# A planner's dependency on two bias additions is loosened, and its table of urgencies replaced

## The chip, the cores and the metric

The kernel runs on one core of one Trainium2 chip. The metric is device time in microseconds (us), start to end of one execution; lower is better. Three runs of the kernel before gave 688.78, 688.41 and 686.49 us, so its median is 688.41 us.

## The reference

Two layers are computed on 2048 tokens of 640 channels, both gated by a vector `c` (adaptive layer norm), everything in float32. Cut to what matters:

```python
mod = (silu(c) @ w_mod).reshape(1, 6, 1, 640)
sa, ca, ga, sb, cb, gb = (mod[:, i] for i in range(6))
h = layernorm(x) * (1 + ca) + sa                  # x is A_q
ks = short causal convolution of k, 4 taps per channel
kv = ks * v
y  = long causal convolution of kv with ssm_k, per channel, by FFT, + kv * ssm_D
x  = x + ga * (h * y)
h  = layernorm(x) * (1 + cb) + sb
r  = relu(h @ w1 + b1)                            # 640 -> 1728
x  = x + gb * ((r * r) @ w2 + b2)                 # 1728 -> 640
```

## The kernel before

**Two stages.** The first stage, the long convolution, goes over five blocks of 128 channels (index b, 0 to 4). For each block the keys and values are loaded (`kn`), turned on TensorE (`kt`, `vt`), put through the short convolution on VectorE (`ks`), multiplied (`km`) and stored to DRAM as `kv_d` (`kst`); from there they come back in another layout (`lx`) as the tile `p`, which has an `ssm_k` half as well (`lh`). Matmuls with constant matrices then do a Fourier transform in steps: `pa` (64 x 64 or 128 x 64 pieces of `p`), `x` and `h` (spectra), products on VectorE (`mul`), their sums on GpSimd (`comb`), the way back (`qp`, then turns `t`, then `y`), and the residual (`fin`). Blocks overlap: the loads and turns of block b+1 stand between the steps of block b. Early in the first stage twenty groups of four transposes of the identity (`warm`), which compute nothing, are laid between TensorE's steps.

The second stage, the MLP, goes over eight chunks of 256 tokens (index n, 0 to 7). `tokens(n)` loads a chunk (`lx1`), takes its statistics (`st2`), normalizes it on ScalarE into `mtmp` (`hat`, one instruction for each half of 128 tokens) and turns it into `xt`, split in a high and a low part, since matmuls run on a reduced float32 (`xt`; the low part is a subtraction on GpSimd, on VectorE for chunk 0). Then there are 14 steps f over the hidden size: five products each (`f1`), bias, ReLU and square (`mid`, on ScalarE and VectorE, split again into high and low parts in `hring` or `w_W`), and four products into accumulators (`f2`). At a chunk's end VectorE multiplies the accumulators by the gate row (`out`) and adds them to the chunk's tile `x_n`, one half on GpSimd (`out` 2), one on VectorE (`out` 5), and the result is stored. In chunk 0 the 28 weight tiles are loaded (`lw`) and split (`wh`, `wl`).

**The two additions.** The second bias is multiplied by the gate once, `row1b = b2 * gate` (`gb2row` in the trace), on GpSimd. For each chunk GpSimd then adds this row to both halves of the chunk's tokens, in place, so two instructions for each chunk, 128 x 640 each. The trace shows them as `x<-x,gb2row`. They need the chunk's tile and must follow the reading of it by `hat`; the chunk's end needs them.

**What sets the order.** Nothing in the code's text order does. Every operation is recorded as a node, a planner inside the kernel (`Graph.order`) lays the nodes in time by rough costs, and each engine's instructions are emitted in that order. The planner picks, for each engine that is free, the ready node with the highest priority. A node's priority is the number that the table `URGE` has for its key and its place among the nodes of that key, in tenths of a microsecond; nodes without a number get one from the longest way to the end:

```python
n.told = i < len(table)
if n.told:
    n.prio = table[i] / 10
elif self.urge:
    n.prio -= LAST
```

The table covers the first stage and chunks 0 and 1; chunks 2 to 7 go almost wholly without. A node is ready when its `deps` are done. Most of these follow from the tiles that it reads and writes; some are set by hand, and those stand in the planner alone. [...] The code around the change (`tokens(0)` has just been recorded, so that the nodes with key `("xt", 0)` are chunk 0's transposes and splits):

```python
tokens(0)
later = {}
g.key = ("gate", 0)
mul(pool, row1b, row1b, row0b)
...
            mlp_middle(n, f)
            if f == 5:
                later[n] = g.nodes[-1].id
            mlp_back(n, f)
        for i in range(2):
            add(pool, X1t[n][:, i], X1t[n][:, i], row1b)
            g.nodes[-1].deps.add(later[n])
        mlp_out(n)
```

All instructions of both stages are issued from one line of a recording helper, so the trace gives them the line L444, and one goes by tiles.

Of the kernel before, what the change touches and what calls it, by code (L numbers as in the profile page):

```python
# [509 lines left out]
def ssm_mlp_kernel(  # L510
# [115 lines left out]
    g = Graph()  # L626
# [672 lines left out]
    def mlp_out(n):  # L1299
# [18 lines left out]
        if n < NC - 1:  # L1318
# [4 lines left out]
        ("b1", 0): [-2365, -2340],  # L1323
        ("comb", 0): [-473, -502, -505, -495, -516, -519, -559, -570, -227, -556, -600, -613, -607, -628, -621, -650,
            -657, -619, -664],
        ("comb", 1): [-939, -957, -941, -936, -967, -960, -971, -1018, -1013, -1030, -1032, -1058, -1065, -1084,
            -1080, -1235, -1228, -1133, -1182],
        ("comb", 2): [-1531, -1509, -1534, -1503, -1541, -1517, -1569, -1576, -1562, -1588, -1581, -1664, -1671,
            -1654, -1685, -1720, -1678, -1734, -1727],
        ("comb", 3): [-1945, -1981, -1969, -1948, -1966, -2021, -2001, -1990, -2004, -2026, -2032, -2059, -2056,  # L1330
            -2070, -2077, -2114, -2087, -2146, -2179],
        ("comb", 4): [-2384, -2378, -2394, -2387, -2825, -2412, -2416, -2431, -2442, -2450, -2475, -2482, -2485,
# [20 lines left out]
        ("fin", 0): [-1310, -1315, -1318, -1350, -1314, -1428, -1337, -1414, -1254, -1442],  # L1353
        ("fin", 1): [-1431, -1464, -1462, -1427, -1692, -1600, -1595, -1879, -1615, -1849],
        ("fin", 2): [-1852, -1858, -1856, -1848, -1912, -2059, -1955, -1999, -1995, -1827],
        ("fin", 3): [-2265, -2269, -2294, -2272, -2613, -2487, -2340, -2688, -2418, -2124],
        ("fin", 4): [-2635, -2642, -2639, -2645, -2664, -2964, -2715, -2950, -2717, -2898],
        ("gate", 0): [-2564, -2502, -2637, -2440, -2414, -2474, -2517, -2568, -2317, -2487, -2228, -2585, -2263,
            -2706, -2724, -2574, -2734, -2916, -2675, -2677, -2682, -2674, -2694, -2780],
        ("gb", 0): [-211, -221, -242, -252],  # L1360
        ("gi", 0): [-526, -339, 54, -592],
        ("h", 1): [-562, -577, -577, -604, -544, -956, -1031, -1033, -1019, -1023, -984, -1044, -1018, -1065, -944,
            -1129],
        ("h", 2): [-1169, -1237, -613, -1243, -1508, -1521, -1527, -1538, -1545, -1554, -1569, -1580, -1604, -1637,
            -1653, -1678],
        ("h", 3): [-1792, -1806, -1792, -1823, -2055, -1837, -2083, -2013, -2007, -2041, -2381, -2052, -2098, -2090,
            -2131, -2113],
        ("h", 4): [-2339, -2359, -2077, -2371, -1728, -2394, -1997, -2422, -1925, -2461, -2522, -2477, -2223, -2175,
            -2642, -2513],
        ("hat", 0): [-2700, -3202],  # L1370
        ("hat", 1): [-3488, -3440],
        ("hat", 2): [-3500, -3500],
# [25 lines left out]
        ("kst", 0): [-51, -277, -247, -252],  # L1398
        ("kst", 1): [-491, -593, -651, -725],
        ("kst", 2): [-1168, -720, -144, -1300],  # L1400
        ("kst", 3): [-1404, -1579, -839, -1069],
        ("kst", 4): [-1816, -2000, -1443, -2127],
        ("kt", 0): [4270, 4415, 1158, 3311],
        ("kt", 1): [-384, -383, -561, -691],
        ("kt", 2): [-642, -830, -1372, -1354],
        ("kt", 3): [-1303, -1334, -1494, -1642],
        ("kt", 4): [-1672, -1771, -1868, -1988],
        ("lgb", 0): [-115, -181],
        ("lgi", 0): [-454, -549, -526],
# [203 lines left out]
    kn = {}  # L1613
# [127 lines left out]
    for n in range(NC):  # L1741
        for f in range(NF):
# [7 lines left out]
            if f == 5:  # L1750
                later[n] = g.nodes[-1].id
# [33 lines left out]
```

## Time and profile before

| | |
|---|---|
| median of 3 runs | 688.41 us |
| the profiled execution | 691.67 us, of which the span from first to last instruction is 689.9 us |
| TensorE (PE) busy | 661.6 us, 96% of the span, 6825 matmul instructions |
| VectorE (DVE), ScalarE (ACT), GpSimd (POOL) busy | 417.7, 314.1 and 263.1 us |
| granted TensorE clock | 0.992 |
| mean DMA rate | 105 GB/s, most of it in the first 260 us |

Times in the trace are us from the span's start. PE is the engine that ends last nearly everywhere. The first stage fills about the first 283 us, the MLP the rest; the slices of the profile show the DMA engines busy in the first and nearly idle in the second. "Idle before" in a row is the time in which an engine had nothing to run, with what ended it. SP is the queue that issues nearly all DMAs, in order.

### The profile page before, as it was taken

The numbers are of one execution on the slowest core, as the hardware profiler recorded it, in microseconds if no ns is written. First come the engines' busy times: TensorE is split into PE (matmuls) and PEld (weight loads), VectorE is DVE, ScalarE is ACT, GpSimd is POOL, SyncE is SP. The second block draws the span as 40 slices with busy tenths as digits, with TensorE's granted clock in tenths as the row PEclk, the third lists the DMA queues.
The fourth block names the chain that finished last, engine by engine and source line by source line (L and its number), as shares of the span: only waits on it lengthen the run. The fifth ranks groups of instructions, "written<-read, shape, count | busy, mean of one in ns | idle before, by whom it ended". The sixth has DMA issues, their size and how long they took to land.

```text
span 689.9 us, 16413 instructions
## 1 busy us (share of the span) xinstructions
PE 661.6 (96%) x6825; PEld 598.6 (87%) x6825; DVE 417.7 (61%) x810; ACT 314.1 (46%) x650; POOL 263.1 (38%) x332
## 2 busy tenths in 40 slices
PE   9998889999999899999999999999999999999996
PEld 8987589879879687799989999899899899899996
DVE  2768559789699486676456562654653562662542
ACT  2765748876656655556225242243232242242220
POOL 2439448868958385354022211311211220310110
PEclk9999999999999999999999999999999999999998
DMA  9897898998776364072020200110020110200011
GB/s 241 224 310 257 210 264 197 238 240 215 203 185 163 89 157 150 20 211 75 1 77 0 77 1 1 23 55 1 0 77 1 39 39 1 52 26 1 1 39 38
DMA packets 108430, 72.45 MB, mean 105 GB/s; under 512 B 48514, under 2 KB 95810, under 8 KB 108356
## 3 DMA queue, kind: packets, MB, share of 16 engines
q1 hardware_dynamic: 106304, 70.80, 39.1%
q8 instruction: 53, 0.87, 0.5%
q10 hardware_dynamic: 1988, 0.61, 0.4%
q14 instruction: 21, 0.17, 0.1%
q0 software_dynamic: 64, 0.01, 0.0%
HBM read 56.98 MB, written 14.42 MB: 103 GB/s over the span
## 4 chain that ended last, share of the span: by engine, by line
PE 82%; DVE 9%; DMA 4%; issue 2%; ACT 2%; DVEq 0%; SPq 0%; POOL 0%; ACTq 0%; POOLq 0%
PE ps L444 82%; DVE mtmp L444 3%; DVE KV L444 3%; DMA p<-kv_d 2%; DVE hring L444 1%; DMA kv_d<-KV 1%; DVE x L444 1%; DVE wx L444 1%; DMA x<-x_d 1%; DMA out_dram<-x 1%; ACT a L444 0%; DVE s L444 0%; ACT KV L444 0%; ACT mtmp L444 0%; DVE w_W L444 0%
## 5 line engine op out<-in xcount | busy, mean ns | idle before, releaser
L444 PE MATMUL ps<-xt,w_S 128*128 128x256 f32 (+1 forms) x935 | 175.9, 330 | 4.0 <-DVE mtmp L444 3.0
L444 PEld LDWEIGHTS ps<-xt,w_S 128*128 128x128 f32 x935 | 140.9, 188 | 18.7 <-DVE mtmp L444 5.0
L444 PE MATMUL ps<-w_S,hring 128*128 128x320 f32 x648 | 109.9, 311 | 0.0
L444 ACT ACTIVATE mtmp<-ps,b1t 128x256 f32<-128x256 f32 (+1 forms) x112 | 50.1, 471 | 123.8 <-PE ps L444 121.0
L444 PEld LDWEIGHTS ps<-w_S,hring 128*128 128x128 f32 x648 | 99.1, 188 | 2.1
L444 DVE TENSOR_TENSOR mtmp<-ps,mtmp 128x256 f32<-128x256 f32 (+1 forms) x99 | 40.2, 418 | 75.7 <-ACT mtmp L444 75.4
L444 PE MATMUL ps<-a,gb 128*64 128x128 f32 x1260 | 75.7, 275 | 2.0 <-ACT a L444 1.4
L444 PEld LDWEIGHTS ps<-a,gb 128*64 128x64 f32 x1260 | 69.2, 137 | 8.8 <-ACT a L444 1.9
L444 POOL TENSOR_TENSOR xt<-xfs,xt 128x256 fp32r<-128x256 f32 x35 | 28.0, 807 | 119.6 <-ACT xt L444 119.4
L444 PEld LDWEIGHTS ps<-cst,p 64*64 64x64 f32 (+1 forms) x1792 | 60.1, 137 | 11.0 <-issue 4.7
L444 PE MATMUL ps<-cst,p 64*64 64x64 f32 (+1 forms) x1792 | 65.3, 247 | 4.4 <-DMA p<-kv_d 2.2
L444 DVE TENSOR_TENSOR hring<-mtmp,hring 128x256 fp32r<-128x256 f32 x74 | 41.7, 570 | 45.4 <-ACT hring L444 44.8
L444 POOL TENSOR_TENSOR wx<-wx 128x256 f32<-128x256 f32 x80 | 59.0, 755 | 7.5 <-DVE wx L444 6.2
L444 ACT ACTIVATE hring<-mtmp 128x256 fp32r<-128x256 f32 x74 | 30.4, 415 | 68.0 <-PE ps L444 47.2
L444 POOL TENSOR_TENSOR x<-mtmp,x 128x640 f32<-128x640 f32 (+1 forms) x9 | 12.9, 1435 | 125.2 <-DVE mtmp L444 125.2
L444 ACT ACTIVATE a<-ps 128x512 f32<-128x512 f32 x72 | 41.1, 616 | 35.9 <-PE ps L444 35.7
L444 PE MATMUL ps<-w_S,w_W 128*128 128x320 f32 x312 | 53.4, 311 | 1.5 <-DVE w_W L444 1.5
L444 PEld LDWEIGHTS ps<-w_S,w_W 128*128 128x128 f32 x312 | 47.8, 188 | 2.7 <-DVE w_W L444 1.7
L444 DVE SCALAR_TENSOR_TENSOR mtmp<-mtmp 128x256 f32<-128x256 f32 x91 | 46.7, 527 | 1.6
L444 DVE TENSOR_TENSOR wx<-ps,wx 128x512 f32<-128x512 f32 x64 | 40.9, 682 | 8.6 <-PE ps L444 6.1
L444 PE MATMUL ps<-gi,wx 64*128 64x128 f32 x640 | 40.4, 277 | 2.4 <-DVE KV L444 1.5
L444 POOL TENSOR_TENSOR mtmp<-mtmp 128x256 f32<-128x256 f32 (+1 forms) x21 | 14.8, 707 | 71.3 <-ACT mtmp L444 71.3
(141 smaller groups left out, 1097.6 us busy)
## 6 DMA issues: line engine op xcount, KB each, us to landing
wm<-in_w_mod_dram SPq DMA_DIRECT2D x25, 320.0 KB, 4.7
p<-in_A_ssm_k_dram SPq DMA_DIRECT2D x20, 256.0 KB, 4.8
KV<-in_A_k_dram SPq DMA_DIRECT2D x20, 256.0 KB, 5.0
KV<-in_A_v_dram SPq DMA_DIRECT2D x20, 256.0 KB, 5.2
p<-kv_d SPq DMA_DIRECT2D x20, 256.0 KB, 4.9
xp<-in_A_q_dram SPq DMA_DIRECT2D x10, 512.0 KB, 7.3
q<-in_A_q_dram SPq DMA_DIRECT2D x7, 640.0 KB, 5.4
out_dram<-x SPq DMA_DIRECT2D x14, 320.0 KB, 3.8
```

The source lines that it names most:

```text
L444: fn(*real, **{k: a.real() if isinstance(a, View) else a for k, a in kw.items()})
```

## The change

In the planner, the two additions of chunks 0 and 1 now have chunk 0's last `xt` node as their extra dependency, the one that the product `b2 * gate` had already; those of chunks 2 to 7 have none beyond their data. And the table is replaced: every entry of the first stage and of chunks 0 and 1 has another number. No instruction is added, removed or altered; each engine has as many of each kind as before.

```diff
     URGE = {
-        ("b1", 0): [-2365, -2340],
+        ("b1", 0): [-2693, -1653],
...
     tokens(0)
-    later = {}
+    first = max(n.id for n in g.nodes if n.key == ("xt", 0))
     g.key = ("gate", 0)
     mul(pool, row1b, row1b, row0b)
-    g.nodes[-1].deps.add(max(n.id for n in g.nodes if n.key == ("xt", 0)))
+    g.nodes[-1].deps.add(first)
...
             mlp_middle(n, f)
-            if f == 5:
-                later[n] = g.nodes[-1].id
             mlp_back(n, f)
         for i in range(2):
             add(pool, X1t[n][:, i], X1t[n][:, i], row1b)
-            g.nodes[-1].deps.add(later[n])
+            if n < 2:
+                g.nodes[-1].deps.add(first)
         mlp_out(n)
```

What that does to the queues is shown at three places. The first is GpSimd's queue around the ends of chunks 1 to 3. `x_2_...` is the tile of chunk 2, `xt_...` the low parts of the next chunk's `xt` (`xt_4849` in the old rows and `xt_4838` in the new are chunk 3's), the 64-row product belongs to a chunk's last step. Before:

```order
L444 TENSOR_TENSOR xt_4849<-xfs,xt_4849 128x256 x5
L444 TENSOR_TENSOR mtmp<-mtmp 64x256
L444 TENSOR_TENSOR x_2_4436<-mtmp,x_2_4436 128x640
L444 TENSOR_TENSOR x_3_4736<-x_3_4736,gb2row 128x640 x2
L444 TENSOR_TENSOR xt_5332<-xfs,xt_5332 128x256 x5
```

Now:

```order
L444 TENSOR_TENSOR x_1_1729<-mtmp,x_1_1729 128x640
L444 TENSOR_TENSOR x_3_4737<-x_3_4737,gb2row 128x640 x2
L444 TENSOR_TENSOR xt_4838<-xfs,xt_4838 128x256 x5
L444 TENSOR_TENSOR mtmp<-mtmp 64x256
L444 TENSOR_TENSOR x_2_4380<-mtmp,x_2_4380 128x640
```

The two additions of chunk 3 stood behind the end of chunk 2, and stand now ahead of chunk 3's low parts. The same move is made in chunks 2 to 7.

The second place is GpSimd's queue at the start of the MLP; `mtmp<-mtmp` are the squares of chunk 0, `x_0` and `x_1` the tiles of chunks 0 and 1. Before:

```order
L444 TENSOR_TENSOR gb2row<-gb2row,gbrow 128x640
L444 TENSOR_TENSOR mtmp<-mtmp 128x256 x6
L444 TENSOR_TENSOR x_0_1734<-x_0_1734,gb2row 128x640 x2
L444 TENSOR_TENSOR mtmp<-mtmp 128x256
L444 TENSOR_TENSOR xt_3983<-xfs,xt_3983 128x256 x2
```

Now:

```order
L444 TENSOR_TENSOR gb2row<-gb2row,gbrow 128x640
L444 TENSOR_TENSOR x_0_1698<-x_0_1698,gb2row 128x640
L444 TENSOR_TENSOR mtmp<-mtmp 128x256 x3
L444 TENSOR_TENSOR x_0_1698<-x_0_1698,gb2row 128x640
L444 TENSOR_TENSOR mtmp<-mtmp 128x256 x4
L444 TENSOR_TENSOR x_1_1729<-x_1_1729,gb2row 128x640
```

One addition of chunk 0 stands now directly behind the product that makes the row, ahead of the first squares, and chunk 1's additions, which stood behind chunk 0's end, begin seven squares later.

The third place is SP's queue at the last return of `kv_d` in the first stage. `p_2004` and `p_2018` are block 4's tile, `w1s` and `w2s` weight tiles of the MLP, `xp` the tokens for the last residual. Before:

```order
L643 DMA xp_2819<-in_A_q_dram 64x16x128 x2
L643 DMA kv_d<-KV 128x512
L643 DMA p_2004<-kv_d 128x8x64
L643 DMA w1s_3032<-in_B_w_dram 128x5x128
L643 DMA w2s_3035<-in_B_w_dram 128x640
L643 DMA w1s_3039<-in_B_w_dram 128x5x128
L643 DMA w2s_3042<-in_B_w_dram 128x640
L643 DMA p_2004<-kv_d 128x8x64 x3
```

Now:

```order
L643 DMA xp_2828<-in_A_q_dram 64x16x128 x2
L643 DMA kv_d<-KV 128x512
L643 DMA p_2018<-kv_d 128x8x64 x2
L643 DMA w1s_3045<-in_B_w_dram 128x5x128
L643 DMA p_2018<-kv_d 128x8x64 x2
```

Three of the four weight loads that stood between the pieces of block 4's tile have moved behind them.

More of the change, by code (lines that the diff above doesn't have):

```diff
@@ L1356, in ssm_mlp_kernel @@
[L1356 to L1371, printed above, removed]
@@ new lines, in ssm_mlp_kernel @@
+        ("comb", 0): [-494, -492, -506, -496, -513, -574, -567, -557, -517, -550, -543, -580, -581, -610, -617, -654,
+            -647, -665, -672],
+        ("comb", 1): [-967, -969, -955, -962, -973, -1006, -974, -976, -1013, -1020, -1049, -1089, -1026, -1068,
+            -1075, -1133, -1110, -1140, -1183],
+        ("comb", 2): [-1511, -1507, -1554, -1500, -1561, -1521, -1514, -1547, -1586, -1603, -1596, -1624, -1617,
+            -1664, -1671, -1721, -1691, -1731, -1697],
+        ("comb", 3): [-1962, -1958, -2102, -1972, -1979, -2006, -1999, -2049, -2021, -2027, -2034, -2083, -2076,
+            -2114, -2090, -2133, -2148, -2167, -2174],
@@ new lines, in ssm_mlp_kernel @@
+        ("gate", 0): [-2556, -2379, -2601, -2383, -2017, -2372, -2468, -2375, -1518, -2386, -2436, -2282, -568,
+            -2698, -2756, -3279, -2650, -3370, -2198, -2478, -3317, -2161, -2380, -2800],
+        ("gb", 0): [-165, -107, -114, -202],
+        ("gi", 0): [-685, -691, -535, -673],
+        ("h", 1): [-582, -593, -591, -674, -937, -953, -959, -968, -974, -985, -991, -1011, -1042, -1053, -1059,
+            -1085],
+        ("h", 2): [-1268, -1266, -1939, -1299, -928, -1510, -940, -185, -924, -530, 210, -1624, -1365, -1630, -1209,
+            -1658],
@@ new lines, in ssm_mlp_kernel @@
+        ("h", 3): [-1520, -1816, -2446, -1973, -1514, -1839, -1488, -1954, -1514, -1567, -1955, -2048, -1725, -2379,
+            -2183, -2190],
+        ("h", 4): [-2654, -2393, -1746, -2379, -1327, -2384, -1117, -2423, -1016, -2454, -1015, -2472, -2262, -2491,
+            -1311, -2510],
+        ("hat", 0): [-2737, -2671],
+        ("hat", 1): [-2828, -2815],
+        ("hat", 2): [-3500, -3500],
[25 rows of a table added]
+        ("kst", 0): [1094, 1317, 2035, 1095],
+        ("kst", 1): [-449, -685, -602, -754],
+        ("kst", 2): [-1024, -1161, -1264, -1313],
@@ new lines, in ssm_mlp_kernel @@
+        ("kst", 3): [-1498, -1274, -1334, -1698],
+        ("kst", 4): [-1433, -1853, -1806, 63],
+        ("kt", 0): [1434, 403, 69, -1119],
+        ("kt", 1): [84, -1026, 160, -738],
+        ("kt", 2): [-788, -813, 23, 251],
+        ("kt", 3): [-2561, -1184, -2302, -3670],
+        ("kt", 4): [-1294, -1552, -1525, -1507],
+        ("lgb", 0): [-16, -140],
+        ("lgi", 0): [-483, -533, -450],
[36 rows of a table added]
+        ("lxp", 0): [-935, -693],
+        ("lxp", 1): [-1111, -1033],
+        ("lxp", 2): [-1516, -1471],
@@ new lines, in ssm_mlp_kernel @@
+        ("mul", 2): [-1484, -1491, -1495, -1496, -1546, -1515, -1568, -1561, -1582, -1594, -1651, -1644, -1665,
+            -1658, -1674, -1688],
+        ("mul", 3): [-1951, -1944, -1968, -1960, -1986, -1402, -1999, -2006, -2072, -2049, -2083, -2087, -2128,
+            -2122, -2136, -2146],
+        ("mul", 4): [-2394, -2358, -2377, -2402, -2413, -2414, -2431, -2437, -2456, -2435, -2498, -2501, -2497,
+            -2511, -2532, -2530],
+        ("out", 0): [-3285, -3502, -3349, -3278, -3262, -3274, -3664, -3740],
[8 rows of a table added]
@@ new lines, in ssm_mlp_kernel @@
+        ("pac", 4): [-2660, -2360, -2295, -2321, -2134, -2329, -2252, -2259, -2541, -2541, -2461, -2272, -2372,
+            -2346, -2235, -2241],
+        ("pra", 0): [-1074, -1085, -1091, -1047, -1089, -1059, -1064, -1067, -1288, -1157, -1162, -1042, -1069,
+            -1107, -1118, -1064],
+        ("pra", 1): [-1173, -1294, -1183, -1152, -1372, -1315, -1310, -1298, -1305, -1289, -1206, -1206, -1347,
+            -1352, -1339, -1252],
+        ("pra", 2): [-1576, -1615, -1581, -1662, -1579, -1621, -1573, -1639, -1611, -1712, -1606, -1620, -1607,
+            -1704, -1576, -1577],
@@ new lines, in ssm_mlp_kernel @@
+        ("pra", 3): [-2007, -2027, -1997, -1993, -2002, -2032, -2059, -2021, -2075, -2079, -2054, -2020, -2037,
+            -2070, -2084, -2121],
+        ("pra", 4): [-2185, -2256, -2260, -2164, -2195, -2195, -2148, -2408, -2170, -2180, -1990, -2168, -2232,
+            -2190, -2215, -1912],
+        ("prm", 0): [-1131, -1056, -1293, -1147],
+        ("prm", 1): [-1383, -1343, -1281, -1405],
+        ("prm", 2): [-1613, -1725, -1742, -1734],
+        ("prm", 3): [-2061, -2032, -2166, -2099],
@@ new lines, in ssm_mlp_kernel @@
+        ("prm", 4): [-1989, -2157, -1919, -1951],
+        ("prp", 0): [-1248, -1116, -1312, -1160],
+        ("prp", 1): [-1446, -1442, -1324, -1450],
+        ("prp", 2): [-1757, -1773, -1885, -1805],
+        ("prp", 3): [-2129, -2071, -2194, -2197],
+        ("prp", 4): [-2278, -2220, -2260, -2281],
+        ("qp", 0): [-600, -632, -584, -610],
+        ("qp", 1): [-777, -1185, -935, -970],
+        ("qp", 2): [-1514, -1827, -1900, -2372],
+        ("qp", 3): [-1759, -1969, 921, -291],
+        ("qp", 4): [-2166, -2698, -3288, -3008],
@@ new lines, in ssm_mlp_kernel @@
+        ("qpc", 0): [-298, -540, -660, -666, -671, -675, -703, -910],
+        ("qpc", 1): [-1037, -1019, -1178, -1214, -1151, -1167, -1228, -1238],
+        ("qpc", 2): [-1599, -1587, -1675, -1681, -1748, -1754, -1762, -1768],
+        ("qpc", 3): [-1914, -2244, -1962, -1968, -2026, -2032, -2132, -2144],
+        ("qpc", 4): [-2652, -2509, -2319, -2570, -2732, -3291, -2489, -2585],
[26 rows of a table added]
+        ("warm", 0): [1525, 1417, -573, -129, -715, 1521, 1524, 1103, 16, -618, -234, 1526, -230, -642, 1413, 1532,
[38 rows of a table added]
```

99 lines of the change are left out of this document (19 added, 80 removed), and 356 rows, old and new, of the table URGE.

## The prediction

> **What bounds the kernel now.** I read the page first, then the busy time by stretches of 20 us, then the chain of waits and the timeline at the stretches with gaps.
>
> ```profile
> span 689.9 us, 16413 instructions
> ...
> PE 661.6 (96%) x6825; PEld 598.6 (87%) x6825; DVE 417.7 (61%) x810; ACT 314.1 (46%) x650; POOL 263.1 (38%) x332
> ...
> PE 82%; DVE 9%; DMA 4%; issue 2%; ACT 2%; DVEq 0%; SPq 0%; POOL 0%; ACTq 0%; POOLq 0%
> ```
>
> TensorE is the bound almost throughout: 82% of the chain that ended last is its own work. The change removes no instruction, so it can win only in the 689.9 - 661.6 = 28.3 us in which PE had nothing to run, or lose by adding to them. Where these stand:
>
> ```profile
> 60.00:80.00 20.00, 16.55 (x179) 13.02 (x180) 16.69 (x40) 14.89 (x27) 14.11 (x18) 1.00 0.87 271
> 80.00:100.00 20.00, 16.53 (x189) 12.95 (x189) 9.57 (x19) 9.89 (x20) 6.33 (x14) 0.91 0.98 248
> ...
> 220.00:240.00 20.00, 17.42 (x476) 13.32 (x476) 9.80 (x17) 13.81 (x31) 9.07 (x9) 0.91 0.49 121
> ...
> 280.00:300.00 20.00, 19.17 (x144) 18.02 (x143) 13.06 (x21) 13.86 (x30) 9.01 (x9) 1.00 0.24 64
> ...
> 340.00:360.00 20.00, 18.55 (x114) 16.84 (x113) 11.28 (x20) 4.55 (x12) 4.96 (x3) 1.00 0.19 49
> ...
> 440.00:460.00 20.00, 19.58 (x119) 17.54 (x118) 14.60 (x33) 7.10 (x16) 5.44 (x3) 1.00 0.23 66
> ...
> 480.00:500.00 20.00, 18.93 (x118) 17.39 (x116) 10.85 (x17) 4.41 (x11) 5.03 (x3) 1.00 0.00 1
> 500.00:520.00 20.00, 19.43 (x125) 18.14 (x126) 9.91 (x29) 7.04 (x17) 2.29 (x3) 1.00 0.24 66
> ...
> 540.00:560.00 20.00, 19.13 (x116) 17.19 (x115) 12.34 (x31) 6.70 (x15) 4.66 (x3) 1.00 0.24 67
> ...
> 580.00:600.00 20.00, 19.69 (x121) 17.80 (x119) 10.73 (x20) 4.40 (x11) 5.45 (x3) 1.00 0.10 21
> 600.00:620.00 20.00, 19.64 (x127) 18.34 (x128) 12.21 (x33) 8.70 (x20) 3.35 (x4) 1.00 0.15 47
> ```
>
> The columns are PE, weight load, DVE, ACT, POOL. Idle PE is 20 less the first: 3.45 and 3.47 us at 60 to 100, 2.58 at 220, and in the MLP, from 340 on, 1.45 + 0.42 + 1.07 + 0.57 + 0.87 + 0.31 + 0.36 = 5.05 us, all at ends of chunks; its other stretches are nearly full.
>
> **The chunks' ends (the dependency).** The group of additions, and one chunk's end, with rows of PE, DVE and POOL only:
>
> ```profile
> L444 POOL TENSOR_TENSOR x<-x,gb2row 128x640 f32<-128x640 f32 x16 | 28.9, 1828 | 0.0
> ```
>
> ```profile
> 492.19 2.13 DVE L444 SCALAR_TENSOR_TENSOR mtmp<-mtmp 128x256 f32<-128x256 f32 x2
> 492.42 1.62 POOL L444 TENSOR_TENSOR x<-mtmp,x 128x640 f32<-128x640 f32 x1 [16.31 <-DVE mtmp L444]
> ...
> 494.00 3.46 POOL L444 TENSOR_TENSOR x<-x,gb2row 128x640 f32<-128x640 f32 x2
> 494.24 3.50 DVE L444 TENSOR_TENSOR hring<-mtmp,hring 128x256 fp32r<-128x256 f32 x2
> ...
> 499.31 0.42 DVE L444 TENSOR_TENSOR w_W<-mtmp,w_W 128x256 fp32r<-128x256 f32 x1
> ...
> 500.12 0.62 PE L444 MATMUL ps<-xt,w_S 128*128 128x512 f32 x2 [1.19 <-DVE mtmp L444]
> ```
>
> The additions never wait once they are at the queue's head (idle 0.0): they run behind the chunk's last sum on POOL. While they run, VectorE's two subtractions take 3.50 us where one alone takes 0.42, so each addition holds VectorE by 3.50 / 2 - 0.42 = 1.33 us, and PE then waits 1.19 us for VectorE. The sum ahead of them (492.42) does the same once, and it stays. Sixteen additions hold VectorE at worst by 16 x 1.33 = 21 us; at the ends the price to PE is the 5.05 us. The new order takes the additions of chunks 1 to 7 away from there. Two of three holds go, and as PE's cover takes up the first of them, I take 4.0 of the 5.05 as gone; the ends of the range are 5.05 and 1.0.
>
> Where they go, beside the next chunk's turns:
>
> ```profile
> 400.40 1.73 ACT L444 ACTIVATE mtmp<-x,nm,rs 128x640 f32<-128x640 f32 x2
> ```
>
> ```profile
> 403.28 0.54 DVE L444 TENSOR_SCALAR xfs<-ps,cbs 128x256 f32<-128x256 f32 x1 [1.72 <-PE ps L444]
> ...
> 406.33 0.54 DVE L444 TENSOR_SCALAR xfs<-ps,cbs 128x256 f32<-128x256 f32 x1 [0.62 <-PE ps L444]
> ```
>
> ```profile
> 404.36 0.74 POOL L444 TENSOR_TENSOR xt<-xfs,xt 128x256 fp32r<-128x256 f32 x1 [13.78 <-ACT xt L444]
> ```
>
> The first addition can start when the first `hat` ends, 400.40 + 1.73 / 2 = 401.3, and two of 1.62 (the sum's row) end at 404.5, where the first low part started at 404.36; POOL had been idle for 13.78 us. So the low parts hardly move, and queued behind the additions is nothing else. VectorE has gaps of 1.72 and 0.62 us there, which take up one hold of 1.33 each in part. I charge 1.0 in all, some 0.2 us for each of the six chunks and so near the lower end, as both gaps are close to a hold's size; the range is from 0 to 6 x (2 x 1.33 - 1.72) = 5.6. Term: -4.0 + 1.0 = -3.0, from -5.0 to +4.6.
>
> The Trainium skill (SBUF — State Buffer, Who interferes with whom) says that a VectorE instruction with two SBUF inputs and a GpSimd instruction that reads SBUF block each other wholly, whichever comes first, and that one with at most one SBUF input, outside VectorE's two-port modes, doesn't contend. The 3.50 us agree for the two-input subtraction, and moved additions would by that rule hold VectorE as long at the new place as at the old; the term would then be -4.0 + 5.6 = +1.6, if no gap took any of it. That case is among the rivals, worked out there from rows.
>
> **The start of the MLP.**
>
> ```profile
> 276.13 0.69 DVE L444 TENSOR_TENSOR up<-ps,up 128x512 f32<-128x512 f32 x1 [0.72 <-PE ps L444]
> ...
> 278.31 0.62 DVE L444 COPY wx<-ps 128x512 f32<-128x512 f32 x1
> ...
> 282.43 1.54 POOL L444 TENSOR_TENSOR gb2row<-gb2row,gbrow 128x640 f32<-128x640 f32 x1 [0.28 <-ACT gbrow L444]
> 283.31 0.94 DVE L444 TENSOR_TENSOR xt<-xfs,xt 128x256 fp32r<-128x256 f32 x1 [0.63 <-ACT xt L444]
> ...
> 284.31 3.95 PE L444 MATMUL ps<-xt,w_S 128*128 128x256 f32 x31 [0.47 <-DVE xt L444]
> ```
>
> In the new order VectorE's half of the first `hat` stands ahead of the product and the copy of the first two rows (0.69 + 0.62 = 1.31 us) and of statistics of chunk 1. So the 0.83 us that PE lost at 280 to 300 can go, and about as much ahead of it: -1.7 at best. Against this, an addition follows the row's product at once: two holds more for the low parts on VectorE, 2 x 1.33 = +2.7 at worst. PE has `f1` of three steps to run in any order meanwhile, which hides most. I take -1.0, nearer the gain.
>
> **Block 4's last pieces.**
>
> ```profile
> 226.08 1.63 PE L444 MATMUL ps<-cst,p 64*64 64x64 f32 x96
> ...
> 230.41 0.88 PE L444 MATMUL ps<-ident,q 128*128 128x128 f32 x6 [2.34 <-issue]
> ```
>
> PE stood for 2.34 us with no data missing, just after it had run 96 instructions in 1.63 us. I read this as instructions that came late. The new SP order has three weight loads fewer in the burst of transfers there and puts the small matmuls less densely. Gain 0 to 2.34; I take 1.2, the middle.
>
> **Block 1's return from DRAM.**
>
> ```profile
> 69.28 1.10 PE L444 MATMUL ps<-ident,KV 128*128 128x128 f32 x8
> ...
> 70.31 2.06 PE L444 MATMUL ps<-gi,wx 64*128 64x128 f32 x32
> ```
>
> ```profile
> 72.05 0.40 DVE s L444
> ...
> 73.88 0.80 DVE s L444 x2
> ...
> 75.50 4.51 DMA kv_d<-KV
> ...
> 80.03 7.39 DMA p<-kv_d
> ...
> 87.46 8.94 PE ps L444 x128
> ```
>
> The last piece of block 1 must be turned (69.28), convolved, stored (75.50) and fetched again (80.03) before PE can go on at 87.46; this is the largest single wait, and no cover is left on PE. The new PE order puts these turns behind the matmuls of 70.31, so they start 2.06 to 2.9 us later; VectorE's queue in turn no longer has statistics between the convolution's steps (0.40 + 0.80 us and two short sums). With 2.06 - 1.2 and a little less waiting ahead of it I take +0.4, from -1.2 to +2.9.
>
> **Shape changes.** The PE queue changes matmul shape 121 times, it was 103.
>
> ```profile
> 15.07 1.29 PEld L444 LDWEIGHTS ps<-ident,KV 128*128 128x128 f32 x12 [0.17 <-issue]
> ```
>
> Each change leaves weight loading idle for up to 0.17 us; I take 0.1 of 0 to 0.17. Twelve of the 18 stand ahead of 48 us, among the `warm` transposes that fill waits there, so I count six: +0.6, up to 18 x 0.17 = +3.1. The Trainium skill (TensorEngine Tiling (Array Packing), Key Properties) speaks against the change here: a change of the tiling mode drains TensorE. It gives no time; with a drain of 0.17 us at all 18 the sum below would be 2.5 us higher.
>
> The rest of the first stage and of chunks 0 and 1 is reordered too; PE has the same work there ahead of each landmark (first `x` of each block, first `f1`). I count 0, and 3 us to both sides.
>
> **The sum.** -3.0 - 1.0 - 1.2 + 0.4 + 0.6 = -4.2 us. The profiled execution took 691.67 us, 3.3 above the median of 688.41; on it this gives 687.5, on the median 684.2, which is my number. About 0.3%, or 2.1 us, is what a measurement of this kernel can tell from no change.
>
> **The rivals.**
>
> *The holds are only moved (chance 0.17).* The last sum on POOL, which stays, holds VectorE by itself at each end, and only 1.0 of the 5.05 us goes: term 0, sum -1.2, 687.2 us. For it: the 1.62 us row has VectorE at 2.13 for two instructions. Against: the worse holds are the additions'.
>
> *VectorE is held beside the turns, and PE waits there (0.14).* Each pair costs 2 x 1.33 = 2.7 us on VectorE, the gaps take up 1.72 or 0.62, mean 1.2; the 1.5 left reach PE in chunks 2 to 7: +9.0 in place of +1.0. Sum +3.8, 692.2 us. It decides against the change from about 1.2 us a chunk on (6 x 1.2 + the other terms = +2). For it: the accumulator banks that the turns need are freed by these very VectorE instructions. Against: the two gaps, and that the matmuls behind VectorE have a queue of other work there.
>
> *Blocks 1 and 2 return late (0.11).* The turns behind `qp` cost their full 2.9 us at block 1, and as much at block 2: +2.5 + 2.9, sum +1.2, 689.6 us; with shape changes at 0.17, 692.
>
> *All of it goes well (0.04).* The ends give 5.05 with no new cost, block 4 all 2.34: about 680.
>
> My forecast has 0.54. So faster by over 0.3%: 0.54 + 0.04 = 0.58; within: 0.17 and half of the third rival, 0.22; slower: 0.14 and the other half, 0.20. The range reaches from 678, where all terms are at their best ends (-5.0 - 1.7 - 2.34 - 1.2 + 0 = -10.2), to 692.5, the second rival.
>
> **What would show it.** In the profile after, additions stand at about 401 to 405 and beside each later chunk's turns; at the chunks' ends VectorE's subtractions are back to 0.42 but for one beside the last sum, and idle PE from 340 us on falls from 5 to about 2. If instead `f1` or the turns wait for VectorE just behind the additions, the second rival holds. The first `f1` starts at 281 to 284; if it starts after 286 the first stage is what failed. At 228 the gap of 2.34 has shrunk; the first `pa` of block 1's `p<-kv_d` comes within a microsecond or two of 87.5. I am wrong if PE's idle time grows in stretches of which I said nothing.

## The result, and the profile after

The kernel after takes 683.31 us in the median of 7 runs (681.87 to 684.53), the kernel before 688.54 us on the same chips (7 runs, 684.40 to 690.43): ratio 0.993, with a 95% interval of 0.9903 to 0.9956. That is 5.2 us less, where 4.2 was forecast. The profiled execution took 684.05 us, span 682.2.

The head of the page of the kernel after, and its busy time by stretches of 20 us (PE, weight load, DVE, ACT, POOL, granted clock, DMA share, GB/s):

```profile
span 682.2 us, 16444 instructions
...
PE 659.1 (97%) x6825; PEld 595.3 (87%) x6825; DVE 415.2 (61%) x810; ACT 315.9 (46%) x650; POOL 260.8 (38%) x332
```

```profile
60.00:80.00 20.00, 17.81 (x208) 14.48 (x206) 14.32 (x32) 14.28 (x26) 15.03 (x18) 1.00 0.92 292
80.00:100.00 20.00, 18.94 (x257) 15.02 (x258) 11.99 (x24) 12.75 (x24) 9.07 (x16) 1.00 0.98 260
...
200.00:220.00 20.00, 17.16 (x273) 15.52 (x274) 16.91 (x26) 10.36 (x22) 12.27 (x17) 1.00 0.56 129
220.00:240.00 20.00, 19.91 (x575) 15.84 (x572) 16.97 (x24) 16.67 (x35) 14.99 (x14) 1.00 0.40 93
...
280.00:300.00 20.00, 18.42 (x138) 17.43 (x137) 12.92 (x20) 11.68 (x26) 11.48 (x12) 1.00 0.31 86
...
340.00:360.00 20.00, 20.00 (x125) 18.47 (x124) 11.44 (x29) 7.08 (x16) 3.94 (x3) 1.00 0.24 67
...
480.00:500.00 20.00, 20.00 (x125) 18.55 (x124) 10.35 (x23) 4.92 (x12) 1.68 (x1) 1.00 0.18 40
```

From 340 us on no stretch has idle PE any more until the last matmul; the 5.05 us are gone. At 280 to 300 idle PE has nearly doubled, from 0.83 to 1.58 us. In the first stage the idle time at 60 to 100 has fallen from 6.92 to 3.25 us, the gap at 220 is gone, and there is a new one at 200.

A chunk's end in the kernel after (the timeline of DVE and POOL; the same end that the prediction shows):

```profile
488.94 2.12 DVE L444 SCALAR_TENSOR_TENSOR mtmp<-mtmp 128x256 f32<-128x256 f32 x2
490.99 0.75 DVE L444 TENSOR_TENSOR hring<-mtmp,hring 128x256 fp32r<-128x256 f32 x2
491.66 0.88 DVE L444 TENSOR_TENSOR mtmp<-ps,gbrow 128x320 f32<-128x320 f32 x2
```

```profile
489.10 1.68 POOL L444 TENSOR_TENSOR x<-mtmp,x 128x640 f32<-128x640 f32 x1 [16.32 <-DVE mtmp L444]
```

The two subtractions take 0.75 us, they took 3.50. The sum on POOL still holds VectorE once (2.12 for two instructions), and no PE wait follows. The additions now wait for their chunk's `hat` and stand beside the turns (`xfs` are turned values that VectorE takes from PSUM):

```profile
398.24 3.12 POOL L444 TENSOR_TENSOR x<-x,gb2row 128x640 f32<-128x640 f32 x2 [14.01 <-ACT mtmp L444]
401.32 0.92 POOL L444 TENSOR_TENSOR xt<-xfs,xt 128x256 fp32r<-128x256 f32 x1
```

```profile
399.79 0.55 DVE L444 TENSOR_SCALAR xfs<-ps,cbs 128x256 f32<-128x256 f32 x1 [1.98 <-PE ps L444]
400.25 0.42 DVE L444 TENSOR_TENSOR mtmp<-ps,mtmp 128x256 f32<-128x256 f32 x1
400.58 1.06 DVE L444 TENSOR_TENSOR hring<-mtmp,hring 128x256 fp32r<-128x256 f32 x1
401.57 1.29 DVE L444 SCALAR_TENSOR_TENSOR mtmp<-mtmp 128x256 f32<-128x256 f32 x2
```

Here a pair holds VectorE by 1.06 - 0.42 = 0.64 us, not by two times 1.33: in its first two microseconds VectorE waits for PE or reads PSUM, and those instructions run at their plain 0.55 and 0.42. The row behind (1.29 for two, 0.75 plain) starts at 401.57, when the pair has ended (398.24 + 3.12 = 401.36), and stands beside GpSimd's low part of `xt`, which held VectorE in the kernel before too:

```profile
404.41 0.97 DVE L444 TENSOR_TENSOR hring<-mtmp,hring 128x256 fp32r<-128x256 f32 x1
```

**Which part of the kernel gained.** I cut each trace at two points: the start of the first `f1` of chunk 0, and that of chunk 3.

| trace | first `f1` at | from there to chunk 3 | from chunk 3 to the last `f2` |
|---|---|---|---|
| before | 283.33 | 133.69 | 266.57 |
| after | 281.06 | 133.57 | 261.55 |
| dependency alone | 280.48 | 138.10 | 261.44 |
| urgencies alone | 280.82 | 134.08 | 269.70 |
| before, chunks 2 to 7 freed | 279.43 | 134.54 | 261.37 |
| before, POOL's queue alone | 278.28 | 135.33 | 261.25 |
| after, chunks 0 and 1 later | 281.29 | 132.34 | 261.51 |

The last column splits the kernels cleanly: about 261.4 us wherever the additions of chunks 2 to 7 are free, 266.6 or more where they aren't (the 269.70 come from a profiled execution that took 692.48 us, 3.6 above its kernel's median; a stop of 1.44 us in it is followed by a granted clock of 0.66 at 510 to 515). The first column doesn't split them by table.

### The profile page after: what moved, and what is told of

It is laid out like the page before. It is cut to its first block, busy times and chain, and to the rows that moved or that the text cites. A ratio compares the mean times of both kernels' runs of the same rounds, so it can differ in the third digit from the quotient of the medians.

```text
span 682.2 us, 16444 instructions
## 1 busy us (share of the span) xinstructions
PE 659.1 (97%) x6825; PEld 595.3 (87%) x6825; DVE 415.2 (61%) x810; ACT 315.9 (46%) x650; POOL 260.8 (38%) x332
## 4 chain that ended last, share of the span: by engine, by line
PE 73%; DVE 5%; POOL 3%; issue 1%; ACT 1%; DMA 1%; SPq 0%; DVEq 0%; POOLq 0%
PE ps L444 73%; DVE wx L444 1%; DVE KV L444 1%; POOL wx L444 1%; DMA w2s<-in_B_w_dram 1%; POOL kover L444 1%; DVE xt L444 1%; DVE up L444 1%; ACT up L444 0%; DVE x L444 0%; POOL xp L444 0%; POOL KV L444 0%; ACT KV L444 0%; DVE w_S L444 0%; SPq L643 0%
## 5 line engine op out<-in xcount | busy, mean ns | idle before, releaser
L444 PE MATMUL ps<-a,gb 128*64 128x128 f32 x1260 | 77.3, 275 | 8.2 <-DVE wx L444 2.7
L444 DVE TENSOR_TENSOR hring<-mtmp,hring 128x256 fp32r<-128x256 f32 x74 | 37.0, 503 | 53.5 <-ACT hring L444 53.1
L444 PEld LDWEIGHTS ps<-cst,p 64*64 64x64 f32 (+1 forms) x1792 | 58.2, 135 | 10.8 <-issue 4.2
L444 POOL TENSOR_TENSOR x<-x,gb2row 128x640 f32<-128x640 f32 x16 | 26.1, 1648 | 88.2 <-ACT mtmp L444 73.2
L444 DVE SCALAR_TENSOR_TENSOR mtmp<-mtmp 128x256 f32<-128x256 f32 x91 | 43.4, 490 | 1.8
```

The lines of the kernel that those rows point to most:

```text
L444: fn(*real, **{k: a.real() if isinstance(a, View) else a for k, a in kw.items()})
```

## The experiments

**The dependency alone.** Old table, new dependency.

```diff
-            g.nodes[-1].deps.add(later[n])
+            if n < 2:
+                g.nodes[-1].deps.add(first)
```

> The kernel before with its old table and the new dependency alone; its queues are those of before up to the first steps of chunk 0. Theory A (two separate gains: the additions at the chunks' ends cost PE some 5 us, and the new table's first stage brings the MLP forward by 2.3): this one has the first alone, first f1 at 283.3 as before, idle PE from 340 us on near 0, 688.5 - 5.0 = 683.5, ratio 0.993 of before. Theory B (the gain is the table's, which orders the first stage and chunks 0 and 1 more densely; the holds were covered): 688.5, ratio 1.000, and idle PE from 340 us on stays near 5. By the prediction's own sizes (4.0 gone, 1.0 new) 685.5, ratio 0.996.

Measured: 687.91 us against 687.60, ratio 1.0007 (0.9991 to 1.0024). Neither theory had this. The last column of the table has its whole gain of 5.1 us, and the column before it gives 4.4 back, at the MLP's start. PE and ACT there, then the same stretch by fives:

```profile
291.71 2.35 PE L444 MATMUL ps<-xt,w_S 128*128 128x256 f32 x18
296.47 0.69 PE L444 MATMUL ps<-ident,mtmp 128*128 128x128 f32 x2 [2.41 <-ACT mtmp L444]
```

```profile
292.35 0.40 ACT L444 ACTIVATE hring<-mtmp 128x256 fp32r<-128x256 f32 x1
295.28 0.74 ACT L444 ACTIVATE w_S<-w2s 128x640 fp32r<-128x640 f32 x1 [2.53 <-DMA w2s<-in_B_w_dram]
295.94 0.47 ACT L444 ACTIVATE mtmp<-ps,b1t 128x256 f32<-128x256 f32 x1
```

```profile
290.00:295.00 5.00, 4.06 (x32) 3.69 (x31) 4.48 (x5) 2.66 (x5) 2.71 (x2) 1.00 0.40 101
295.00:300.00 5.00, 3.53 (x15) 3.51 (x16) 2.94 (x6) 3.30 (x8) 0.61 (x1) 0.66 0.79 219
```

It isn't a hold. The old table's numbers for the additions of chunks 0 and 1 were harmless while the old dependency kept them back; without it three of the four stand among the MLP's first steps on GpSimd, and ScalarE's queue now has splits of weights ahead of steps of `mid` that stood ahead of them (because the planner reckons with later squares on GpSimd, I suppose). One of them waits 2.53 us for its weight to land; PE's next turn of chunk 1 waits for the `mid` behind it (for the bank that it frees, I take it), and PE stops 2.41 us. In the five microseconds behind the stop the granted clock is 0.66. With chunks 2 to 7 freed alone (below), ScalarE waits nearly as long for a weight, two splits further on in its queue, and PE doesn't stop:

```profile
298.01 0.74 ACT L444 ACTIVATE w_S<-w2s 128x640 fp32r<-128x640 f32 x1 [2.37 <-DMA w2s<-in_B_w_dram]
```

**The urgencies alone.** New table, old dependency.

```diff
-            if n < 2:
-                g.nodes[-1].deps.add(first)
+            g.nodes[-1].deps.add(later[n])
```

> The new table with the old dependency: the first stage is that of after, the additions of each chunk stand again behind the sum of the chunk ahead of it. Theory A: first f1 at about 280 to 281, idle PE from 340 us on 4 to 5 us, 688.5 - 2.3 = 686.2, ratio 0.997. Theory B: 683.3 as after, ratio 0.993. If the dependency and the table only work together, this and the one with the dependency alone are both near 1.000.

Measured: 688.84 us, ratio 1.002 (1.0 to 1.004). Both theories fall: the table alone brings nothing. The idle PE from 340 us on is back at the ends (1.36 at 340, 1.10 at 480, 1.91 at 500). And the 2.3 us by which the profile of after was ahead at the first `f1` weren't the table's: six traces with the old first stage start it at 278.28 to 283.33 (mean 279.95), six with the new one at 277.67 to 281.60 (mean 280.43). The profile of before was the latest of all twelve.

**Only chunks 2 to 7 freed, old table.**

```diff
-            g.nodes[-1].deps.add(later[n])
+            if n < 2:
+                g.nodes[-1].deps.add(later[n])
```

> The kernel before, with only the additions of chunks 2 to 7 freed; the first stage and chunk 0 are those of before to the instruction, the end of chunk 0 keeps its additions of chunk 1 (0.42 us of idle PE there). Theory A: 688.5 - 5.05 + 0.5 = 684.0, ratio 0.9935. If the holds are as dear beside the turns as at the ends (rival 2 of the prediction, +9.0 in place of +1.0): 688.5 - 4.5 + 8 = 692, ratio 1.005. Theory B: ratio 1.000.

Measured: 684.13 us, ratio 0.9947 (0.993 to 0.9963). Theory A said 684.0. The second rival's 692 us (VectorE held beside the turns in every chunk) are refuted. What is left is at the end of chunk 0, which this kernel doesn't touch (1.46 us idle at 340 to 360), and 0.55 beside chunk 2's turns, where the rival's mechanism does appear once: the pair at its new place holds two of VectorE's subtractions for 3.29 us, and PE waits for the second. POOL, DVE and PE there:

```profile
364.13 3.27 POOL L444 TENSOR_TENSOR x<-x,gb2row 128x640 f32<-128x640 f32 x2 [11.57 <-ACT mtmp L444]
```

```profile
364.39 3.29 DVE L444 TENSOR_TENSOR hring<-mtmp,hring 128x256 fp32r<-128x256 f32 x2 [0.69 <-ACT hring L444]
```

```profile
367.74 0.85 PE L444 MATMUL ps<-w_S,hring 128*128 128x320 f32 x4 [0.55 <-DVE hring L444]
```

**POOL's queue alone, the order of all other engines kept.** In the line that the planner has laid, before it is emitted:

```diff
-    g.emit(g.order())
+    line = g.order()
+    for n in range(2, NC):
+        pair = [o for o in line if o[2].engine == "POOL" and o[2].key == ("f2", n)]
+        line = [o for o in line if o not in pair]
+        at = next(i for i, o in enumerate(line) if o[2].engine == "POOL" and o[2].key == ("xt", n))
+        line[at:at] = pair
+    g.emit(line)
```

> The kernel before; in GpSimd's queue alone the additions of chunks 2 to 7 are laid ahead of their own chunk's first low part of xt, behind the end of the chunk before is nothing; TensorE's, VectorE's, ScalarE's and SP's queues are those of before to the instruction. Freeing these additions in the planner, which reorders TensorE's queue a little too, gave 684.13 against 687.6. Theory A (place: the additions hold VectorE's subtractions at the ends, and beside the turns PE has cover): the 5.05 us of idle PE from 340 us on shrink to the 1.5 us at the end of chunk 0, 687.6 - 3.5 = 684.1, ratio 0.995. Theory C (the gain came from the new order of TensorE's steps): 687.6, ratio 1.000, and idle PE beside the turns instead.

Measured: 683.09 us against 688.00, ratio 0.9932 (0.9908 to 0.9956). TensorE's queue is the old one to the instruction, and the gain is there. So it is where these twelve instructions run on GpSimd that costs or saves the time, not the new order of matmuls. Of idle PE from 340 us on, 1.45 us are left at the end of chunk 0, as expected, and 1.16 beside chunk 2's turns, which weren't.

**Twice as many additions beside the turns.**

```diff
+    for n in g.nodes:
+        if n.engine == "POOL" and n.key[0] == "f2" and n.key[1] >= 2:
+            n.calls = n.calls * 2
```

> The kernel after, with each addition of chunks 2 to 7 issued twice in a row, so the tokens get the second bias's row twice there: four additions beside each chunk's turns in place of two, all queues else the same. A hold is 1.33 us, so VectorE loses up to 6 x 2 x 1.33 = 16 us more. If PE's cover at the turns is large (theory A): 683.3 still, ratio to before 0.993 to 0.995, no idle PE from 340 us on. If the prediction's 1.0 us for the pair was a cover nearly used up (its second rival, a wait of 1.5 us a chunk from the second pair on): 683.3 + 6 x 1.5 to 6 x 2.7 = 692 to 699, ratio 1.007 to 1.017.

Measured: 688.19 us, ratio 1.0003 (0.9985 to 1.0021), some 5 us above after, so 0.8 for each chunk: between the two theories. The timeline of DVE and PE at chunk 3's turns:

```profile
398.25 3.48 DVE L444 SCALAR_TENSOR_TENSOR mtmp<-mtmp 128x256 f32<-128x256 f32 x2
...
402.12 0.61 PE L444 MATMUL ps<-xt,w_W 128*128 128x512 f32 x2 [1.16 <-DVE mtmp L444]
```

In the order of after the cover at the turns takes one pair for nothing and not a second one; in the old order even one pair costs 0.55 us beside chunk 2's turns, as seen above. The rival was wrong in its dose, not in its kind.

**One input in place of two.** In the kernel before, the additions of chunks 1 to 7 are replaced when the queues stand.

```diff
+    for n in g.nodes:
+        if n.engine == "POOL" and n.key[0] == "f2" and n.key[1] >= 1:
+            (fn, op, (o, a, b), kw), = n.calls
+            n.calls = [(nc.gpsimd.tensor_scalar, op, (o, a, 1.0, None), dict(op0=ALU.mult))]
```

> The kernel before, its queues unchanged; the additions of chunks 1 to 7 are replaced by a GpSimd instruction of the same size with one tile as input (the tokens times 1.0), so the second bias's row is left out of these chunks. The question is what holds VectorE at the ends. If any GpSimd instruction on these tiles does it for as long as it runs: the group's duration sets the price, idle PE from 340 us on stays 4 to 5 us if it takes 1.6 us or so as the addition does, 687.6, ratio 1.000. If two inputs on GpSimd's side are needed: the subtractions are back to 0.42 us beside it, idle PE near 1, 683.6, ratio 0.994. The Trainium skill (SBUF — State Buffer, Who interferes with whom) names every GpSimd instruction that reads SBUF, and so the first.

Measured: 681.00 us, ratio 0.9897 (0.9873 to 0.992). DVE and POOL at the same chunk's end:

```profile
487.56 1.27 DVE L444 TENSOR_TENSOR hring<-mtmp,hring 128x256 fp32r<-128x256 f32 x2
```

```profile
487.32 3.77 POOL L444 TENSOR_SCALAR x<-x 128x640 f32<-128x640 f32 x2
```

The GpSimd instructions are even longer (1.89 us each), at the same place, and the subtractions beside them take 1.27 us instead of 3.50. So it isn't GpSimd's being busy that holds VectorE; the form with two tiles as inputs does it, and the form with one hardly. (The two differ in the kind of instruction as well, `tensor_tensor` and `tensor_scalar`; this run doesn't part that from the number of inputs.) From the first `f1` to the last `f2` this kernel takes 393.61 us, before takes 400.26: the additions' price at all ends was at least 6.65 us, by one trace of each. That is more than the 5.05 us of idle PE, and the median is 2.6 us below the 683.6 that the second theory had reckoned from them. The Trainium skill (SBUF — State Buffer, Who interferes with whom) has a two-input VectorE instruction contend with any GpSimd instruction that reads SBUF; here the one-input form slowed it by (1.27 - 0.75) / 2 = 0.26 us on average, the two-input form by (3.50 - 0.75) / 2 = 1.38, so the measurement parts what the rule puts together.

**Chunks 0 and 1 later, new table.** The four additions wait in the planner for chunk 0's sixth step. The first two of the texts below are for the two measurements of this kernel, the third is for the kernel after, measured once more beside the second.

```diff
-                g.nodes[-1].deps.add(first)
+                g.nodes[-1].deps.add(sixth)
```

> The kernel after, with the additions of chunks 0 and 1 held back in the planner to chunk 0's sixth step, so that none stands right behind the product of the row; chunks 2 to 7 stay free. In after the first of them holds VectorE's low part of xt by 1.35 us, and PE stops for 1.35 us right behind it and 1.00 ahead. If that stop is the addition's, 1.35 us go: 683.3 - 1.35 = 682.0, ratio to before 0.991. If PE waits there for the weights or ScalarE in any case, or makes up for the stop later, nothing changes: 683.3, ratio 0.993.

> The kernel after with the additions of chunks 0 and 1 behind chunk 0's sixth step, once more: if it is really 1.2 us ahead, as the stop at 282.4 to 285.9 in after and the 132.34 against 133.57 us from the first f1 to chunk 3's say, 0.9913 of before and 682.0 where after has 683.2. If the two medians (681.35 and 683.31) differed by chance: both 0.992 to 0.993.

> The kernel after, once more, beside the next on the same chip: 0.993 of before, 683.0 to 683.5. Its first f1 starts anywhere between 277.5 and 283 if the first stage scatters as the traces of before's order did (278.3 to 283.3 at the same queues), which would mean that the 2.3 us by which its profile was ahead there were none of the table's.

Measured: 681.35 us at first (ratio 0.9914, 0.989 to 0.9938); beside the kernel after 683.00 (0.9917, 0.9891 to 0.9942) against 682.64 for after (0.9917, 0.9897 to 0.9937). In after an addition stands beside two low parts of `xt` on VectorE, which take 2.10 us (POOL and DVE); in this kernel they take 0.75, so the addition held them by 1.35:

```profile
283.65 1.68 POOL L444 TENSOR_TENSOR x<-x,gb2row 128x640 f32<-128x640 f32 x1
```

```profile
283.52 2.10 DVE L444 TENSOR_TENSOR xt<-xfs,xt 128x256 fp32r<-128x256 f32 x2
```

```profile
283.75 0.75 DVE L444 TENSOR_TENSOR xt<-xfs,xt 128x256 fp32r<-128x256 f32 x2
```

The stop of PE behind it is gone too: PE's rows of after, then of this kernel:

```profile
282.19 2.40 PE L444 MATMUL ps<-xt,w_S 128*128 128x256 f32 x18 [0.50 <-DVE xt L444]
285.68 2.54 PE L444 MATMUL ps<-xt,w_S 128*128 128x256 f32 x19 [1.08 <-DVE xt L444]
```

```profile
282.42 5.86 PE L444 MATMUL ps<-xt,w_S 128*128 128x256 f32 x47 [0.50 <-DVE xt L444]
```

From the first `f1` to chunk 3 it takes 132.34 and 132.29 us in its two traces, after takes 133.57 and 133.53. So the 1.2 us are there in both pairs of traces where they arise, but the first stage scatters by more (at about 201 us both traces of this kernel stop for 3.6 us, after's two for 2.36 and 1.31), and the whole runs don't show them: by the medians I can't say that this kernel beats the one after.

**The same on the old table.** `sixth` for chunks 0 and 1, chunks 2 to 7 free.

```diff
-            g.nodes[-1].deps.add(later[n])
+            if n < 2:
+                g.nodes[-1].deps.add(sixth)
```

> The old table, with the additions of chunks 0 and 1 behind chunk 0's sixth step and those of chunks 2 to 7 free: the dependency of the change, but for the place at the MLP's start. The dependency alone gave 687.9 and had 3.62 us of idle PE at 280 to 300; freeing chunks 2 to 7 alone gave 684.13 and had 1.46 + 0.55 us idle at 340 to 380, where chunk 0 ends. If each stall is worth its length: 684.13 - 1.5 to 2.0 = 682.4, ratio 0.992, the MLP free of idle PE but for 0.4 at its start. If the old table needs its additions of chunk 1 where they stood: 684 to 688. The new table with the same dependencies gave 681.35 (0.9914); a value as low would say that the table is worth nothing here.

Measured: 683.64 us, ratio 0.9933 (0.991 to 0.9956). This is the dependency alone with another place in the planner for four instructions, and 4.3 us better, with no stop of PE at 296: their place at the MLP's start is what the dependency alone lost by. It has 1.13 us of idle PE at 300 and 0.55 at 360 that the new table with the same dependency hasn't, and takes 395.89 us from the first `f1` to the last `f2` where that takes 393.85. So the new table is worth some 2 us in chunks 0 to 2, by these traces, once the additions are free; the medians (683.64 against 681.35 and 683.00) don't settle it.

**Where the gap of 2.34 us comes from.** The old order, with 1 or 7 transposes for 4 in each of the twenty `warm` groups.

```diff
+    for n in g.nodes:
+        if n.key[0] == "warm":
+            n.calls = n.calls[:1]               # the other kernel: n.calls + n.calls[:3]
```

> The kernel before, its order unchanged, with one transpose in place of four in each of the twenty warm groups: 60 transposes fewer, each a weight load and a matmul, so everything behind stands 120 instructions earlier in TensorE's queue. In five traces of the old order a gap of 1.79 to 2.34 us stands before the same matmul, the third of the eight turns of q behind the 96 small matmuls of block 4, whenever that comes. Theory F (the queue's instructions are fetched in pieces of fixed size, and the border of a piece falls on the dense 96): the gap is gone at this matmul or stands elsewhere, 220 to 240 has under 1 us idle. Theory D (what is late there comes from block 4's transfers or from the turns themselves): the gap stays before the same matmul, 2 us. The total says little, since the start of the kernel changes too: 684 to 692.

> As the kernel before, with seven transposes in each warm group in place of four: everything behind stands 120 instructions later in TensorE's queue. Theory F: no gap before that matmul, or a shorter one. Theory D: the gap of 1.8 to 2.3 us stays. The warm groups cost up to 60 x 0.1 = 6 us where nothing else was waited for: 686 to 695 in all.

One run of each: 691.32 us, and 696.38, which is above the range that was expected; the start of the kernel differs, and only the gap counts. PE's timeline with one transpose, then with seven:

```profile
229.01 0.69 PE L444 MATMUL ps<-cst,p 64*64 64x64 f32 x30
230.44 1.26 PE L444 MATMUL ps<-cst,p 64*64 64x64 f32 x66 [0.74 <-issue]
231.62 1.09 PE L444 MATMUL ps<-ident,q 128*128 128x128 f32 x8
```

```profile
232.99 0.81 PE L444 MATMUL ps<-cst,p 64*64 64x64 f32 x38
235.57 1.14 PE L444 MATMUL ps<-cst,p 64*64 64x64 f32 x58 [1.78 <-issue]
236.64 1.09 PE L444 MATMUL ps<-ident,q 128*128 128x128 f32 x8
```

Theory F holds, and to the instruction. Before, the gap stands behind 96 + 2 matmuls. With 60 matmuls more in front it stands behind 38, so 60 earlier in the work; with 60 fewer behind 30, so 68 earlier, and 68 + 60 = 128. The gap stands at fixed places of TensorE's queue, 128 pairs of weight load and matmul apart, 256 instructions. One sign of theory F didn't come: 220 to 240 still has 1.60 and 1.78 us idle, since the gap moved by less than 2 us of work and stayed in that stretch.

## Why the prediction was right, and where it wasn't

The number was right (683.31 against 684.2, well inside 678 to 692.5) and so was the mechanism that carried most of it. Term by term:

- **The chunks' ends** (-4.0): too small. From chunk 3 on the gain is 266.57 - 261.55 = 5.0 us, and chunk 0's end gave its 1.45 as well: 6.4 in all, more than the 5.05 that I had put as the bound. The step that failed is reading the price off PE's idle column: from 420 us on that column had 3.60 us, and the time fell by 5.0. The other 1.4 stand in PE's rows as busy time. The kernel with POOL's queue alone has before's TensorE queue to the instruction, and gains 266.57 - 261.25 = 5.3 us from chunk 3 on; laid matmul by matmul beside before, it gains them at these same ends and, to within 0.1 us, nowhere else. At the end that the prediction shows, before and then that kernel have, from the first of 31 matmuls (the stop of 1.19 us stands in before among them) to the two behind them:

```profile
494.25 4.68 PE L444 MATMUL ps<-xt,w_S 128*128 128x256 f32 x26
...
501.02 0.51 PE L444 MATMUL ps<-xt,w_S 128*128 128x512 f32 x2
```

```profile
489.89 5.03 PE L444 MATMUL ps<-xt,w_S 128*128 128x256 f32 x28
494.76 0.61 PE L444 MATMUL ps<-w_S,hring 128*128 128x320 f32 x3
495.21 0.52 PE L444 MATMUL ps<-xt,w_S 128*128 128x512 f32 x2
```

From start to start that is 6.77 us against 5.32, so this stop costs 1.45 us where the idle column has 1.19. A matmul counts as busy past the point where the next one can start: the row of 28 ends at 489.89 + 5.03 = 494.92, and the row behind it starts at 494.76, without a stop. So each stop is longer than its idle time by some 0.16 us, and the matmuls right behind it come a little late as well.
- **The new cost beside the turns** (+1.0): none, in this order. One pair fits into the cover; the doubled pair shows that the next would cost 0.8 a chunk. The second rival rested on that, and its price of 1.5 was for a load that the change doesn't put there: I took two full holds a pair where 0.64 us were measured at chunk 3. With the old table chunk 2's subtractions had two full holds, and PE waited 0.55 us. A slip in the prediction: its +1.6 is said to hold if no gap took any of a hold, but the 5.6 in it has a gap of 1.72 us taken off already; without that it is 6 x 2.66 = 16 us. The first rival (holds only moved) is refuted by the 0.75 us at the ends.
- **The MLP's start** (-1.0): wrong in sign. Half of what I named as the worst case there happened, one addition held `xt`'s low part, and it costs 1.2 us, as the kernel with later additions shows. VectorE's earlier half of `hat` brought nothing that I can find behind it: even with the additions later, chunks 0 to 2 take 132.34 us, which is before's 133.69 less the 1.45 at chunk 0's end.
- **Block 4's last pieces** (-1.2): the reading as late instructions was right, the conclusion that the gap would shrink wasn't. At 220 to 240 it is gone (0.09 idle), and another stop for instructions stands at 202, in block 3's work:

```profile
201.69 1.42 PE L444 MATMUL ps<-a,gb 128*64 128x128 f32 x22 [2.36 <-issue]
```

- **Block 1's return** (+0.4) and **shape changes** (+0.6): not separable. With -1.2 they made -0.2 for the first stage; the two orders' means differ by 280.43 - 279.95 = +0.5 us, less than either scatters (3.9 and 5.1 us). The return came earlier than before in the profile (idle at 60 to 100 fell from 6.92 to 3.25), but the old order's other traces come back earlier too: 2.36 us of idle PE at 80 to 100 with chunks 2 to 7 freed, where the profile of before has 3.47.

So the sum is -6.4 + 1.2 + 0 = -5.2 us, by the traces all of it in the MLP, for the forecast's -4.2. Two misses, 3.4 too little at the ends with their new cost taken in and 2.2 too much at the MLP's start, mostly cancel in the total; that it came so close is luck in part. Some of the 5.2 may be the granted clock's: it is 0.998 in the mean of 13 runs of after and 0.997 in 56 of before, and the runs with 0.999 take 682.6 and 686.6 us in the mean (7 and 17 runs), 4.1 apart. Of the marks that I had set, the additions' places, the ends, the first `f1` at 281 to 284, block 1's first `pa` (86.16 us) and the vanished gap at 228 came as said; PE's idle time grew at 202, and by 1.3 and 1.8 us at 100 to 120 and 140 to 160, of which I had said nothing.

## What to carry to other kernels

When a wait is loosened in a planner, look at what the old wait was keeping away: the same dependency gained 5 us at the chunks' ends and, under a table of urgencies that had never had to decide there, lost 4 at the MLP's start, on an engine that it doesn't touch. An instruction on a side engine costs by what it stands beside, so move it beside work that reads PSUM or waits anyway, and count the holds from a row of that place. What a stop costs is read from start to start beside a trace without it, not from the idle column alone. Before a gain in one trace of a stretch is believed, lay a second trace of the same queues beside it.

## What the runs showed of the hardware

**Instructions come in pieces of 256.** The two `warm` kernels show it by the shift of the gap, and the page of after by its DMA queues (packets, MB, share):

```profile
q8 instruction: 53, 0.87, 0.6%
```

Fifty-three packets of 16.4 KB are about as many as TensorE's 2 x 6825 instructions make at 256 each (53.3); that this queue is TensorE's I take from the number. It costs where small pairs run faster than the next piece comes, as I read it: 96 of the 64 x 64 matmuls took 1.63 us, and six traces of the old order stop 1.79 to 2.34 us before the same matmul. The Trainium skill (Runtime: NRT & Kernel Launch, Instruction fetch mechanics) gives the same size, 256 instructions in a block, and calls the cost of crossing a border mostly hidden; in this kernel the stops that I found at such places stand within the dense small matmuls or shortly behind them (at 202 in after, 21 matmuls behind 96 of them).

**A stop of PE can cost more than its length.** Behind the 2.41 us stop of the dependency alone the clock is 0.66 for five microseconds, which takes another 0.34 x 5 = 1.7 us. A narrower window shows it at half (the clock is the third number from the end):

```profile
296.30:299.80 3.50, 3.33 (x13) 3.31 (x14) 1.65 (x4) 2.08 (x6) 0.61 (x1) 0.51 0.92 260
```

The runs agree: the mean granted clock of that kernel's 12 runs is 0.9947, and 0.9973 in the 29 runs of before beside them, which is 1.8 us of 688, about one such dip more in each run. The profile of before has such a dip behind block 1's return:

```profile
85.00:90.00 5.00, 2.96 (x35) 2.54 (x36) 3.73 (x8) 0.60 (x1) 0.00 (x0) 0.87 0.67 146
90.00:95.00 5.00, 5.00 (x76) 4.93 (x74) 0.67 (x2) 3.20 (x6) 0.00 (x0) 0.79 1.06 350
```

The traces of the same queues with the dependency alone and with chunks 2 to 7 freed have 1.00 there: whether a stop of 2 to 3 us is followed by a dip differs from run to run (after's stop of 2.36 at 202 wasn't). In the old order the dip at 220 to 240 stands in all but one of six traces (0.91 over the 20 us). The prediction costed gaps by their length alone. The Trainium skill (TensorE: Matmul & The Clock Gate, What's actually happening) has the clock halved after an idle window of about 3.4 us; half the clock for 3.4 us would be the same 1.7 us, an estimate from that page, though the stop of 2.41 us that brought it here is shorter than the window.
